# A fused block-sparse attention and low-rank mixer kernel: casts of U and V and the changeover reordered, and q, k, v of the later head pairs loaded by casting transfers

## The chip, the cores and the metric

One Trainium2 chip, one core. The core has a matrix engine (PE, with its weight loads shown apart as PEld), a vector engine (DVE), a scalar engine for activations (ACT), GpSimd (POOL) and SyncE (SP), which here only issues transfers. Each engine works through its own queue in order. Transfers issued by SP or ACT go out on hardware queues, those issued by POOL on a software queue, whose descriptors POOL's own cores write (SWDGE); all of them run on the same 16 DMA engines. A casting transfer reads one number type and writes another.

The metric is the device time of one execution in microseconds. Before the change: median 285.85 us of 8 runs, from 284.97 to 288.19.

## The reference

The shapes are batch 4, 8 heads, 768 positions, head dimension 64; U is 768 x 32, V 32 x 768, w_ch1 512 x 2048, w_ch2 2048 x 512. All are float32.

```python
scores = scale * np.matmul(q, k.transpose(0, 1, 3, 2))
mask = np.abs(blk_i - blk_j) <= 1        # blocks of 32
mask = mask | (blk_i == 0) | (blk_j == 0) | (blk_i == n_blocks - 1) | (blk_j == n_blocks - 1)
...                                      # and three sampled blocks for each block of queries
scores = np.where(mask, scores, -1000000000.0)
attn = softmax(scores)
x = np.matmul(attn, v)                   # heads side by side: [4, 768, 512]

h = x.transpose(0, 2, 1) @ U @ V
u = x + h.transpose(0, 2, 1)
return u + np.maximum(u @ w_ch1, 0.0) @ w_ch2
```

The mixer works along the positions, so U and V multiply over the 768 positions; the last line is a two-layer network on each position.

## The kernel before

**Pairs, units, batches.** Two heads form a pair (`i`), so there are 16 pairs, four to a batch. The scores of a pair are computed in nine units (`u`), each with two heads by 512 columns into one "double", a PSUM tile of two banks (`psc`). ACT takes the exponential of a unit from PSUM into `est` in fp16 (line 481). All matrix work is in fp16.

**Loading.** `issue` (line 229) has SP load q, k or v of a pair in float32 into `qld`, `kld`, `vld`, two buffers each; the lines of a pair are 1536 contiguous bytes for each partition and head. `cast` (line 235) has POOL convert them: q and k to `qst` and `kst` (two buffers each), v into `vts`, where every head and position tile has 66 columns, 64 of them of v. q and k must then stand with the head dimension on partitions. For pairs 0 to 5 PE transposes them (`turn_part`, line 918, through PSUM `pturn` and a DVE copy); for pairs 6 to 15 SP issues a DMA transpose (`turn_dma`, line 261).

**Batch 0** (loop at line 1025, pairs 0 to 3) is a fixed order: at each unit the scores, the values of the unit three earlier (`flush_value`), and what `at_unit` (line 945) hangs on the unit. The mask is added within the scores' matmul there. When the values of a pair are complete, DVE normalizes them into `xs` (line 524), POOL casts `xh` (line 542), PE multiplies by `Ut` (`pa`), DVE copies, PE multiplies by `Vt` (`ph`), DVE adds `xf` (line 628), POOL casts `uh` (line 642), and PE transposes it (`puT`, line 694) for the network. Those steps of pair 0 fall on the units 5 to 7 of pair 1 and unit 0 of pair 2. `Ut` and `Vt` are cast by POOL from float32 loads that lie in the memory of w2t; behind them POOL issues the casting loads of w1t (line 421) and w2t (line 429), placed on units by `WLOADS`.

**The changeover** (lines 1078 to 1115) leaves that order: the first three units of pair 4, the last steps of pair 3, and the first w1 rows of batch 0's network, with `fill` as the list of its steps. The two-bank PSUM tiles grow from two to four when the single-bank pools `pav` and `ps` are given up (`more_doubles`). `put_off` holds the two full `xf` additions of pair 3.

**The stream** (from line 1183) is a planner that runs while the program is built. It keeps estimated clocks for PE, ACT, DVE and POOL (`clk`), and at each step gives PE the next thing whose inputs are due: a unit of scores, the values of a pair (`pav`), the two mixer products, or a step of the network (`pt` for w1 with the relu into `tT`, `pch` for w2). Exponentials, masks (line 502: a multiplication by DVE in batches 1 to 3), relus and additions are placed on ACT and DVE by those clocks. `run_on("pool", us)` advances the planned clock of POOL, and `mask_mul` reckons 1.25 us for a mask if POOL's clock is ahead of DVE's and 0.69 otherwise. Each engine's order is fixed by the time that the kernel runs. `unit_sides` (line 1043) hangs the loads of pair i+3, the casts of pair i+2 and the DMA transposes of pair i+1 on the units of pair i. SP also issues the DMA transposes of `uh` (line 677) and the stores of the result (line 777), whose tile `of` has one buffer.

Of the kernel before, what the change touches and what calls it, by code (L numbers as in the profile page):

```python
# [11 lines left out]
FP16 = mybir.dt.float16  # L12
# [5 lines left out]
P = 128  # L18
# [3 lines left out]
def kernel(  # L22
# [12 lines left out]
    nc = tc.nc  # L35

    B, H, S, D = q.shape
    BLK = 32
    NB = S // BLK
    T = S // P  # L40
    HD = H * D
    HP = H // 2
# [92 lines left out]
    def later(eng, first, fn, when=None):  # L135
        count[0] += 1
        when = clk["pe"] if when is None else when
        tasks[eng].append((when + LAG, first, count[0], fn))

    def run_engines(t):  # L140
        while True:
            best = None
            for eng in ("act", "dve"):
                for kind in (eng, "any"):
                    for task in tasks[kind]:
                        start = max(clk[eng], task[0])
                        late = 0.15 if kind == "any" and eng == "dve" else 0.0
                        key = (start + late, task[1], task[2])
                        if start <= t and (best is None or key < best[0]):
                            best = (key, eng, kind, task, start)  # L150
            if best is None:
                return
            _, eng, kind, task, start = best
            tasks[kind].remove(task)
            clk[eng] = start
            clk[eng] += task[3](eng)

    def more_doubles(tag, n):
        first[tag].__exit__(None, None, None)
        pool = ctx.enter_context(  # L160
            tc.tile_pool(
                name=f"double{n}p", bufs=1, space=bass.MemoryType.PSUM,
                side="left" if tag == "ps" else "right",
            )
        )
        doubles[n] = (pool, clk["pe"])

    def run_on(eng, us, ready=None):
        clk[eng] = max(clk[eng], (clk["pe"] if ready is None else ready) + LAG) + us
        return clk[eng]  # L170
# [46 lines left out]
    NPAIR = B * HP  # L217
# [11 lines left out]
    def issue(i, names="qkv"):  # L229
        if i >= NPAIR:  # L230
            return
        for nm in names:
            keep(nc.sync.dma_start(out=new_ld(i, nm), in_=src_of(nm, i)))

    def cast(i, nm):
        if i >= NPAIR:
            return
        b, hp = divmod(i, HP)
        ld = lds.pop((i, nm))
        if nm == "v":  # L240
            keep(
                nc.gpsimd.tensor_copy(  # L242
                    out=vts[b % 2][:, 2 * hp : 2 * hp + 2, :, 0:D], in_=ld
                )
            )
            return
        st = stpool.tile([P, T, 2, D], FP16, tag="st" + nm, name=nm + "st")
        keep(nc.gpsimd.tensor_copy(out=st.rearrange("p t h d -> p h t d"), in_=ld))  # L248
        sts[i, nm] = st

    def turn_some(st, pt, t0, t1):
        for t in range(t0, t1):
# [665 lines left out]
    def turn_part(i, nm, part):  # L918

        if part == 0:  # L920
            turning[nm] = pst_tile([P, T, P], FP16, "pturn", tag="ps")
        turn_some(sts[i, nm], turning[nm], 3 * part, 3 * part + 3)
        if part == 1:
            del sts[i, nm]
            pt = turning.pop(nm)
            if i < HP:
                dst = {"q": qa, "k": ka}[nm][i % 2]
                for h in range(2):
                    half_copy(nc.vector.tensor_copy, dst, h, pt, 0, T)
            else:  # L930
                qkT[i, nm] = qkpool.tile([P, T, P], FP16, tag=nm + "T", name=nm + "T")
                keep(nc.vector.tensor_copy(out=qkT[i, nm], in_=pt))
            run_on("dve", 0.48)
# [8 lines left out]
    }  # L942


    def at_unit(i, u):
        if (i, u) in MASKS:
            mask_tiles(MASKS.index((i, u)))
        if i == 0:
            if u == 0:
                warm_pe(1)  # L950
                turn_some(qst, pq, TQ, T)
                turn_some(kst, pk, TK, T)
                for h in range(2):
                    mask_rows("dve", h, pm2[:, 0, 0:QB], QA, S)
                    keep(
                        nc.sync.dma_start(
                            out=qa[1][h][mrows[h], :], in_=qa[0][h][mrows[h], :]
                        )
                    )
                    hot_rows(nc.sync, 1, h, D)  # L960
                for nm, o, pt, t in (("q", qa[0], pq, TQ), ("k", ka[0], pk, TK)):
                    for h in range(2):
                        half_copy(nc.vector.tensor_copy, o, h, pt, t, T)
                for h in range(2):
                    keep(nc.sync.dma_start(out=mvld[h * R : h * R + R], in_=moe_V))
                keep(
                    nc.sync.dma_start(
                        out=uld, in_=moe_U.rearrange("(p t) r -> p (t r)", t=T)
                    )
                )  # L970
                issue(2, "qk")
                cast(1, "q")
                cast(1, "k")
                cast(1, "v")
            if u == 1:
                issue(2, "v")
            if u == 3:
                for r in range(2):
                    at = r * R
                    keep(  # L980
                        nc.gpsimd.tensor_copy(
                            out=Ut[rows[r]].rearrange("p t (h c) -> p t h c", h=2)[
                                :, :, :, at : at + R
                            ],
                            in_=uld[rows[r]]
                            .rearrange("p (t r) -> p t r", t=T)[:, :, None, :]
                            .broadcast_to([D, T, 2, R]),
                        )
                    )
                keep(  # L990
                    nc.gpsimd.tensor_copy(
                        out=Vt[0 : 2 * R, :, :],
                        in_=mvld.rearrange("r (p t) -> r t p", t=T),
                    )
                )
                issue(3)
            if u == 6:
                cast(2, "q")
                cast(2, "k")
                cast(2, "v")  # L1000
            if u == 4:
                turn_part(1, "q", 0)
                turn_part(1, "q", 1)
            if u in (5, 6):
                turn_part(1, "k", u - 5)
            return
        if u == 0:
            issue(i + 3)
        if i == 2 and u == 0:
            for h in range(2):  # L1010
                keep(nc.sync.dma_start(out=Vd[rows[h]], in_=Vt[rows[0]]))
        if (i, u) in WLOADS:
            WLOADS[i, u]()
        if u in (1, 2, 3, 4):
            turn_part(i + 1, "qk"[(u - 1) // 2], (u - 1) % 2)
        if u == 6:
            cast(i + 2, "q")
            cast(i + 2, "k")
        if u == 8:
            cast(i + 2, "v")  # L1020
        for _ in range({0: 1, 5: 2, 6: 1, 7: 1}.get(u, 0)):
            if tails:
                tails.popleft()()
# [19 lines left out]
    def unit_sides(i, u):  # L1043

        if u == 0 and i > HP:
            turn_dma(i + 1, "q")
            turn_dma(i + 1, "k")
        if u in (1, 4, 6):
            issue(i + 3, "qkv"[u // 3])
        if u in (3, 5, 7):  # L1050
            cast(i + 2, {3: "q", 5: "k", 7: "v"}[u])
            run_on("pool", 1.15)

    def next_unit(held_back=False):
        i, u = stream.popleft()
# [16 lines left out]
    def run_fill():  # L1072
        cost, fn, kind = fill.popleft()
        fn()
        state["last"] = clk["pe"]
        return cost
# [3 lines left out]
    for gi in range(3):  # L1080
        next_unit(True)
        if gi == 0:
            flush_value()
            tails.popleft()()
            flush_value()
        if gi == 1:
            flush_value()
            put_off.pop(0)()
        if gi == 2:
            tails.popleft()()  # L1090
            tails.popleft()()
            put_off.pop(0)()


    fill.extend(mlp_steps(0))
# [4 lines left out]
    tails.popleft()()  # L1100
    run_fill()
    tails.popleft()()
    for _ in range(5):
        run_fill()
        run_engines(1e9)
    while put_off:
        put_off.pop(0)()
    more_doubles("pav", 2)
    for nm in "qk":
        for part in range(2):  # L1110
            turn_part(HP + 1, nm, part)
    clk["pe"] = clk["dve"] = max(clk["act"], clk["pe"])
    more_doubles("ps", 3)
    for mask in early:
        later("dve", 3, mask, 0.0)

    opened, credit = 1, 0.0
    uT_at = {b: [] for b in range(B)}
# [115 lines left out]
```

## Time and profile before

| | |
|---|---|
| median of 8 runs | 285.85 us (284.97 to 288.19) |
| the profiled execution | 286.49 us, of which the span of the engines' work is 284.7 us |
| granted PE clock | 1.00 in every stretch |
| transfers of q, k, v by SP | 48 tensors, 384 KB each; median landing 5.2 to 5.6 us |
| casting loads by POOL | w1t 4 x 512 KB written, landing 9.7 us; w2t 4 x 512 KB, 18.5 us |
| DMA transposes | 10 of q, 10 of k, 12 of uh |
| POOL casts of q, k, v | 15.2, 15.1 and 17.3 us busy (15, 15 and 16 casts) |
| DMA share, 94 to 120 us | 0.74 |

Times are in microseconds from the start of the span. A row of a timeline gives start, duration, engine, source line, operation, what it writes and reads, and in brackets how long the engine was idle before it and what ended that. A row of the chain gives start, duration and what the end of the execution hung on at that time. SPq and POOLq stand for an engine's issuing of transfers.

### The profile page before, as it was taken

How to read it: one execution, taken by the hardware profiler on the slowest of the kernel's cores; microseconds unless marked ns; L12 is line 12 of the kernel's file. 1: busy time of each engine (PE TensorE's matmuls, PEld its weight loads, DVE VectorE, ACT ScalarE, POOL GpSimd, SP SyncE). 2: the span in 40 equal slices, each digit the busy share in tenths (PEclk: the TensorE clock that was granted, in tenths of full speed). 3: DMA queues.
4: the chain of work that ended last, by engine and by line, in shares of the span. 5: the costliest groups of instructions: out<-in, count | busy, mean ns of one | idle time of the engine just before them, and what ended most of it. 6: DMA issues, size and time to landing. Idle time of an engine off the chain costs nothing.

```text
span 284.7 us, 8067 instructions
## 1 busy us (share of the span) xinstructions
PE 275.6 (97%) x3509; PEld 164.8 (58%) x3509; DVE 182.6 (64%) x285; ACT 178.7 (63%) x201; POOL 85.5 (30%) x102
## 2 busy tenths in 40 slices
PE   8989999799999999999999999999999999999996
PEld 3567775456565656666656464656565554665443
DVE  5657768767879898986776949886867551000112
ACT  3789997397969685775794757496878200655000
POOL 2459863201526263332242525161102011000000
PEclk9999999999999999999999999999999999999999
DMA  5969999928173596665245383913100303100112
GB/s 165 273 207 351 235 252 268 269 57 223 30 222 51 150 223 230 113 215 116 83 110 141 100 227 105 183 24 63 23 9 2 101 2 104 74 1 2 74 74 75
DMA packets 45235, 37.20 MB, mean 131 GB/s; under 512 B 27144, under 2 KB 42832, under 8 KB 45200
## 3 DMA queue, kind: packets, MB, share of 16 engines
q1 hardware_dynamic: 42024, 32.26, 41.2%
q0 software_dynamic: 2688, 4.19, 8.0%
q8 instruction: 27, 0.44, 0.6%
q10 hardware_dynamic: 488, 0.24, 0.3%
q14 instruction: 8, 0.07, 0.1%
HBM read 27.90 MB, written 6.29 MB: 120 GB/s over the span
## 4 chain that ended last, share of the span: by engine, by line
PE 79%; DMA 7%; ACT 7%; DVE 2%; POOL 2%; issue 1%; SPq 0%; ACTq 0%; DVEq 0%; POOLq 0%
PE pch L174 29%; PE pt L174 29%; PE pav L174 10%; PE psc L174 8%; ACT est L481 7%; DMA kld<-in_k_dram 3%; DMA vld<-in_v_dram 2%; DMA w2t<-in_moe_U_dram 1%; PE pa L174 1%; PE ph L174 1%; DVE tT L721 1%; POOL w1t L421 0%; DVE xh L524 0%; DVE est L502 0%; PE pturn L254 0%
## 5 line engine op out<-in xcount | busy, mean ns | idle before, releaser
L481 ACT ACTIVATE est<-psc 128x1024 f16<-128x1024 f32 x144 | 142.6, 1029 | 45.0 <-PE psc L174 42.6
L174 PE MATMUL pt<-uT,w1t 64*128 64x384 f16 (+1 forms) x896 | 95.6, 324 | 1.0 <-ACT est L481 0.5
L502 DVE TENSOR_TENSOR est<-est,m 128x1024 f16<-128x1024 f16 x108 | 87.1, 835 | 12.1 <-ACT est L481 11.5
L174 PE MATMUL pch<-w2t,tT 64*128 64x512 f16 (+3 forms) x688 | 93.4, 372 | 0.5 <-ACT est L481 0.5
L174 PEld LDWEIGHTS <-w1t 64*128 64x128 f16 (+1 forms) x896 | 46.6, 94 | 37.3 <-PE pt L174 7.0
L174 PEld LDWEIGHTS <-tT 64*128 64x128 f16 (+1 forms) x688 | 38.4, 95 | 38.3 <-PE pch L174 1.6
L719 ACT ACTIVATE tT<-pt 128x768 f16<-128x768 f32 (+1 forms) x50 | 38.6, 779 | 32.0 <-PE pt L174 31.9
L174 PEld LDWEIGHTS <-est 128*128 128x128 f16 x1152 | 41.5, 97 | 11.0 <-issue 5.0
L174 PE MATMUL pav<-vt,est 128*128 128x65 f16 x1152 | 44.5, 193 | 0.2
L774 DVE TENSOR_TENSOR of<-xf,pch 128x1024 f32<-128x1024 f32 (+3 forms) x16 | 15.2, 953 | 43.4 <-PE pch L174 43.3
L174 PE MATMUL psc<-qT,kT 64*128 64x512 f16 (+1 forms) x288 | 40.7, 323 | 0.0
L581 POOL CAST xh<-xs 128x768 f16<-128x768 f32 x12 | 11.1, 923 | 94.9 <-DVE xs L572 84.1
L667 POOL CAST uh<-xf 128x768 f16<-128x768 f32 x12 | 13.4, 1118 | 32.8 <-DVE xf L658 17.2
L174 PE MATMUL psc<-qa,ka 128*128 128x512 f16 (+1 forms) x96 | 22.0, 331 | 0.2
L174 PEld LDWEIGHTS <-kT 64*128 64x128 f16 x288 | 14.5, 94 | 11.0 <-DVE xs L572 0.2
L721 DVE TENSOR_SCALAR tT<-pt 128x768 f16<-128x768 f32 (+1 forms) x18 | 16.3, 910 | 5.1 <-PE pt L174 5.1
L242 POOL CAST vt<-vld 128x768 f16<-128x768 f32 x16 | 17.3, 1082 | 5.8 <-DMA vld<-in_v_dram 5.8
L248 POOL CAST kst<-kld 128x768 f16<-128x768 f32 x15 | 15.1, 1009 | 4.2 <-DMA kld<-in_k_dram 3.0
L248 POOL CAST qst<-qld 128x768 f16<-128x768 f32 x15 | 15.2, 1012 | 2.0 <-DMA qld<-in_q_dram 2.0
L658 DVE TENSOR_TENSOR xf<-xs,ph 128x768 f32<-128x768 f32 x12 | 11.4, 953 | 2.3 <-PE ph L174 2.0
L572 DVE TENSOR_TENSOR xs<-pav,rcp 128x768 f32<-128x768 f32 x12 | 11.5, 958 | 1.2
L570 DVE RECIPROCAL rcp<-pav 128x12 f32<-128x12 f32 x12 | 2.8, 232 | 12.8 <-PE pav L174 12.8
(65 smaller groups left out, 127.3 us busy)
## 6 DMA issues: line engine op xcount, KB each, us to landing
vld<-in_v_dram SPq DMA_DIRECT2D x16, 384.0 KB, 5.2
qld<-in_q_dram SPq DMA_DIRECT2D x15, 384.0 KB, 5.4
kld<-in_k_dram SPq DMA_DIRECT2D x15, 384.0 KB, 5.6
out_dram<-of SPq DMA_DIRECT2D x9, 512.0 KB, 3.3
w1t<-in_moe_w_ch_dram POOLq DMA_DIRECT2D x4, 512.0 KB, 9.7
w2t<-in_moe_w_ch_dram POOLq DMA_DIRECT2D x4, 512.0 KB, 18.5
out_dram<-of SPq DMA_DIRECT2D x5, 256.0 KB, 2.0
qld<-in_q_dram SPq DMA_DIRECT2D x1, 256.0 KB, 2.8
```

The source lines that it names most:

```text
L174: ins = nc.tensor.matmul(out, lhsT, rhs, start=start, stop=stop, skip_group_check=loose)
L242: nc.gpsimd.tensor_copy(out=vts[b % 2][:, 2 * hp : 2 * hp + 2, :, 0:D], in_=ld)
L248: keep(nc.gpsimd.tensor_copy(out=st.rearrange("p t h d -> p h t d"), in_=ld))
L481: keep(nc.scalar.activation(out=est, in_=psc, func=AF.Exp, scale=0.125))
L502: keep(nc.vector.tensor_tensor(out=o, in0=o, in1=m, op=ALU.mult))
L572: nc.vector.tensor_tensor(out=xs.rearrange("p (c j) (h d) -> p c (j h) d", c=2, h=2), in0=pv[:, :, :, 0:D], in1=rcp[:, :, :, None].broadca ...
L581: keep(nc.gpsimd.tensor_copy(out=xh, in_=xs))
L658: nc.vector.tensor_tensor(out=u.rearrange("p (c j) n -> p c j n", c=2), in0=xs.rearrange("p (c j) n -> p c j n", c=2), in1=ph[:, :, 0:HS]. ...
L667: keep(nc.gpsimd.tensor_copy(out=uh, in_=u))
L719: keep(nc.scalar.activation(out=o, in_=i, func=AF.Relu))
L721: keep(nc.vector.tensor_scalar_max(out=o, in0=i, scalar1=0.0))
L774: nc.vector.tensor_add(out=of, in0=xfs[b][:, sc : sc + nsc, n0:n1], in1=pch)
```

## The change

1. The casts of U and V are taken apart. `cast_U` goes from unit 3 to unit 6 of pair 0, ahead of q and k of pair 2; `cast_V`, with the cast of v of pair 2, goes to unit 2 of pair 1. Both turns of k of pair 1 are at unit 6, and the four turns of pair 2 come one unit later than before.
2. `issue(i + 3)` stops with pair 5. For pairs 6 to 15, `load_cast` has POOL issue two casting transfers for each of q, k and v (one for each head), straight into `qst`, `kst` and `vts`. The planner's clock of POOL is no longer advanced for them.
3. q and k of pair 5 are turned by DMA transposes instead of by PE. In the changeover four network steps come after the additions and masks are handed to the planner, and the clocks are set otherwise; the planner's order after that point differs in many places.

```diff
+    def load_cast(i, nm):
+
+        if i >= NPAIR:
+            return
+        b, hp = divmod(i, HP)
+        if nm == "v":
+            o = vts[b % 2][:, 2 * hp : 2 * hp + 2, :, 0:D]
+        else:
+            sts[i, nm] = stpool.tile([P, T, 2, D], FP16, tag="st" + nm, name=nm + "st")
+            o = sts[i, nm].rearrange("p t h d -> p h t d")
+        for h in range(2):
+            keep(nc.gpsimd.dma_start(out=o[:, h], in_=src_of(nm, i)[:, h]))
...
+    def cast_U():
+        for r in range(2):
...
+    def cast_V():
+        keep(
+            nc.gpsimd.tensor_copy(
+                out=Vt[0 : 2 * R, :, :],
+                in_=mvld.rearrange("r (p t) -> r t p", t=T),
+            )
+        )
...
             if u == 3:
-                for r in range(2):
...
                 issue(3)
             if u == 6:
+                cast_U()
                 cast(2, "q")
                 cast(2, "k")
-                cast(2, "v")
             if u == 4:
                 turn_part(1, "q", 0)
                 turn_part(1, "q", 1)
-            if u in (5, 6):
-                turn_part(1, "k", u - 5)
+            if u == 6:
+                turn_part(1, "k", 0)
+                turn_part(1, "k", 1)
             return
-        if u == 0:
+        if u == 0 and i < 3:
             issue(i + 3)
+        if i == 1 and u == 2:
+            cast_V()
+            cast(2, "v")
...
-        if u in (1, 2, 3, 4):
-            turn_part(i + 1, "qk"[(u - 1) // 2], (u - 1) % 2)
+        at = u - 2 if i == 1 else u - 1
+        if at in range(4):
+            turn_part(i + 1, "qk"[at // 2], at % 2)
...
-        if u in (1, 4, 6):
-            issue(i + 3, "qkv"[u // 3])
         if u in (3, 5, 7):
-            cast(i + 2, {3: "q", 5: "k", 7: "v"}[u])
-            run_on("pool", 1.15)
+            load_cast(i + 2, {3: "q", 5: "k", 7: "v"}[u])
...
             put_off.pop(0)()
+            turn_dma(HP + 1, "q")
+            turn_dma(HP + 1, "k")
...
-    for _ in range(5):
-        run_fill()
-        run_engines(1e9)
+    run_fill()
+    clk["act"] = clk["pe"]
+    clk["dve"] = clk["pe"] + 0.5
     while put_off:
         put_off.pop(0)()
-    more_doubles("pav", 2)
-    for nm in "qk":
-        for part in range(2):
-            turn_part(HP + 1, nm, part)
-    clk["pe"] = clk["dve"] = max(clk["act"], clk["pe"])
-    more_doubles("ps", 3)
     for mask in early:
         later("dve", 3, mask, 0.0)
+    for _ in range(4):
+        run_fill()
+    more_doubles("pav", 2)
+    more_doubles("ps", 3)
+    run_engines(clk["pe"])
```

In batch 0's part of the built program POOL's order around the change is: `Ut`, q and k of pair 2, two `xh` of pair 0, `Vt`, v of pair 2, two issues of w1t, q and k of pair 3, `uh`, w1t, `uh`. Before, `Vt` stood behind `Ut`, and the two `xh` behind v of pair 2.

More of the change, by code (lines that the diff above doesn't have):

```diff
@@ L942 @@
     }
+    def cast_U():
+        for r in range(2):
+            at = r * R
+            keep(
+                nc.gpsimd.tensor_copy(
+                    out=Ut[rows[r]].rearrange("p t (h c) -> p t h c", h=2)[
+                        :, :, :, at : at + R
+                    ],
+                    in_=uld[rows[r]]
+                    .rearrange("p (t r) -> p t r", t=T)[:, :, None, :]
+                    .broadcast_to([D, T, 2, R]),
+                )
+            )
+    def cast_V():
+        keep(
+            nc.gpsimd.tensor_copy(
+                out=Vt[0 : 2 * R, :, :],
+                in_=mvld.rearrange("r (p t) -> r t p", t=T),
+            )
+        )
     def at_unit(i, u):
@@ L977, in at_unit @@
             if u == 3:
-                for r in range(2):
[L979 to L995, printed above, removed]
                 issue(3)
             if u == 6:
+                cast_U()
                 cast(2, "q")
                 cast(2, "k")
-                cast(2, "v")
             if u == 4:
```

## The prediction

> **What bounds the kernel now.** I read the page first: the sum of busy time, then the chain of work that ended last.
>
> ```profile
> span 284.7 us, 8067 instructions
> PE 275.6 (97%) x3509; PEld 164.8 (58%) x3509; DVE 182.6 (64%) x285; ACT 178.7 (63%) x201; POOL 85.5 (30%) x102
> PE 79%; DMA 7%; ACT 7%; DVE 2%; POOL 2%; issue 1%; SPq 0%; ACTq 0%; DVEq 0%; POOLq 0%
> ```
>
> PE ends the kernel, but an average hides three stages. From 9.5 to 48 us, batch 0, ACT runs one exponential after another and the chain is ACT's; from 48 to 56 us lies a changeover in which PE and ACT both pause; from 56 us on PE is dense (27.4 of 28.0 us busy in 66 to 94, 32.0 of 32.0 in 150 to 182), so there only less PE work or a stall moves the end. Next, the chain of waits between 17 and 30 us, where batch 0 leaves ACT:
>
> ```profile
> 17.07 5.18 DMA vld<-in_v_dram
> ...
> 22.30 0.83 POOL vt L242
> ...
> 25.20 0.83 POOL qst L248
> 26.03 0.76 POOL kst L248
> 26.79 0.45 POOL uh L642
> 27.23 0.46 POOL w1t L421
> 27.70 0.52 POOL uh L642
> ...
> 28.27 0.34 PE puT L694 x3
> 28.61 0.45 PE psc L174 x2
> ```
>
> The reader should see that POOL, a third busy overall, is here the engine that ends last: the load of v for pair 2 lands, POOL works through its queue without a pause, and PE's transposes of uh (puT) for pair 0, with the scores behind them, wait for its last cast. Then the timelines of POOL and PE at the places that the change rewrites:
>
> ```profile
> 17.80 1.56 POOL L991 CAST Vt<-w2t 64x768 f16<-64x768 f32 x1
> 19.31 0.82 POOL L248 CAST qst<-qld 128x768 f16<-128x768 f32 x1
> 21.31 0.83 POOL L248 CAST kst<-kld 128x768 f16<-128x768 f32 x1 [1.19 <-PE pav L174]
> 20.18 0.34 PE L254 MATMUL pturn<-id,qst 128*128 128x128 f16 x3 [1.03 <-POOL qst L248]
> 54.04 0.51 PE L254 MATMUL pturn<-id,qst 128*128 128x128 f16 x6 [1.58 <-DVE xf L628]
> 55.66 0.39 PE L174 MATMUL psc<-qT,kT 64*128 64x512 f16 x2
> ```
>
> The cast of Vt delays q of pair 2, and PE waits 1.03 us for it. But Vt also fills a pause of POOL, which has to wait for k of pair 2 anyway.
>
> **Part 1, order in batch 0.** Vt's cast (one, 1.56 us) goes from ahead of q and k of pair 2 to behind the two xh of pair 0; the turns of pair 2 come one unit later. I follow POOL's new queue by starts of the rows above. q of pair 2 was issued at 15.06 and landed 3.4 later, so its cast runs at 18.5 and is ready at 19.3; its turn now comes after 20.4, so the 1.03 us wait goes. k was issued at 15.54 and landed 5.6 later, 21.14. From there, start to start: k 0.77, two xh 0.90, Vt 1.51, v 0.77, two issues of w1t 1.21, q and k of pair 3 1.54, uh 0.45, w1t 0.52, uh 0.52: 8.19 us, so the last uh ends at 29.3. Before, it ended at 28.2. PE, freed of its earlier wait, reaches puT a microsecond sooner and waits there longer; what follows (psc, then the exponential that began at 29.13) begins at about 30.2. Price: **+1.1 us**, and both old pauses (ACT's 0.89 before 21.00 and 0.36 before 29.13) lie ahead of this point and bring nothing. Bounds: -1.2 if POOL's order should hurt nobody (0.89 + 0.36 gained), +1.6 if the whole of Vt is added.
>
> **Part 2, the changeover.** Twelve PE transposes for pair 5 (2 x 0.51 us) and two DVE copies (0.56, 0.55) go; two DMA transposes on SP replace them. Their inputs were cast by 42 us and their result is read at pair 5's first scores, past 62 us; the median landing of such transposes is 4.4 and 3.1 us, and SP has only pair 6's loads there, which go. If that cover failed, pair 5's scores would wait. PE's run of pt now goes from 14 to 22 matmuls without the stall on xf. At 0.65 us for eight (chain rows "pt x8") 22 take 1.8 from 51.00: 52.8. The scores then need the PSUM that ph held; DVE reads it in xf, 1.02 us straight behind the uT copy that ended at 51.46: 52.5. So the scores of unit 3 of pair 4 start at 52.9 instead of 55.66: **-2.7 us**. ACT has the four relu halves first (1.75 us from 52.3) and the next exponential at 54.0 instead of 56.1, so it follows. Bounds: -3.0 to -1.0; the low gain if DVE, with nine masks, two half and three whole relus (9 x 0.69 + 1.02 + 2.85) from 51.5 on, delays pair 4's values.
>
> **Part 3, loads that cast.** For pairs 6 to 15, 30 loads leave SP (0.37 to 0.57 us of issuing each) and 30 casts leave POOL (1.08, 1.01, 1.01 us); 60 casting issues of 192 KB read come to POOL.
>
> ```profile
> L429 POOL DMA_DIRECT2D w2t<-in_moe_w_ch_dram x4 | 3.0, 746 | 0.0
> L421 POOL DMA_DIRECT2D w1t<-in_moe_w_ch_dram x4 | 2.3, 572 | 0.0
> q0 software_dynamic: 658, 0.65, 64.2%
> q1 hardware_dynamic: 781, 0.19, 32.7%
> ```
>
> The first two rows are casting issues of 512 and 128 pieces; each new one has 768 (128 partitions x 6 tiles). The slope gives 0.86 us; bounds 0.57 (no slope) and 1.12 (all in proportion). Per pair POOL gives 3.1 us of casts for 5.2 of issues and has, with xh and uh (0.92, 1.12), 7.2 us of work in a pair's 14.3 us (values of pair 4 at 65.94, of pair 13 at 194.55, nine pairs). Behind xh stand four issues, 3.4 us, then uh, whose input came 4.5 us after xh's start at pair 5 (83.40 to 87.93): it fits up to 0.92 us an issue, beyond which uh is late. That moves PE only where uh opens the next batch's w1 rows (pairs 7 and 11).
>
> The last two rows are the DMA view of 42 to 48 us (casting packets, 1024 bytes written: 0.642 x 16 x 6 us / 658 = 94 ns, few short ones among them) and of 75 to 78 us (transposes, 256 bytes: 0.327 x 48 / 781 = 20 ns). Each pair will bring 4608 packets of 128 bytes written, 288 an engine, for 48 of 1536 bytes. Cost of one: between 20 and 94 ns. It is nearest to the 256-byte row in size. The trace's records of single packets say the same more finely: medians of 18 ns for that row, 96 for casting ones of 1024 bytes and 322 for those of 4096 (w1t); the line through the two casting points gives 30 ns at 128 bytes, which I take. Then 8.6 us a pair for loads, 2.9 for three transposes (144 x 20 ns), about 1 for stores: 12.5 of 14.3 us. It fits. The trade-off: k lands later. At pair 8 POOL's xh ends at 84.2, four issues end at 87.6, and with the 5.6 us landing of a plain kld counted from the last issue (86.8) k is there at 92.4, against an SP transpose at 91.78 before. SP then holds its queue 0.6 us, and stores (98.89) and uT (103.63) behind it lose nothing; kT is read 14 us later. DVE's masks that ran at up to 1.31 us beside a POOL cast instead of 0.69 get quicker, without value where PE is dense. Price: **0**.
>
> The Trainium skill, "DMA: Bandwidth & Descriptors", Specifications, speaks against the part: transfers need at least 512 bytes for line rate, below that the engine reads, modifies and writes. The 20 ns row at 256 bytes shows no such penalty for that write. Were it to double 128-byte packets from my 30 ns to 60, an estimate, loads would need 17.3 us a pair and the third rival below would hold.
>
> **The sum**: +1.1 - 2.7 + 0 = -1.6. The profiled execution took 286.49 (span 284.7, 1.8 around it): 284.9. It lies 0.64 above the median of 285.85, so as a median **284.3 us**. About 0.5% (1.4 us, so below 284.4 or above 287.3) is what a measurement of this kernel can tell from no change; my forecast sits on that line.
>
> **Rivals.** *Batch 0 gains too.* POOL's queue is not what holds PE after the move, because casts shorten or PE has work to hide it; then -1.2 - 2.7: 282.0. For it: the 1.03 us wait is real and goes. Against: the chain shows POOL without a pause for 6 us before puT. *The gain is given back.* PE reaches 53 us sooner but the denser first units wait for DVE masks or for relus to free PSUM, so 1.0 stays: 286.0 with Part 1's +1.1. For it: DVE works 10.5 of 13 us in 53 to 66 even before; against: PE then had no pause over 0.25 us. *Loads become the bound* (slower): packets on the 16 DMA engines. It decides from (14.3 + 14.3/10 - 3.9) / 288 = 41 ns a packet, since a lead of about one pair over ten pairs is used up first. At 45 ns, 13.0 + 3.9 = 16.9 a pair: 10 x 2.6 - 14 = +12, 296. For it: 128-byte pieces, v at a stride of 132 bytes, no row of either; against: both nearest rows. *The change doesn't do what it says* is excluded: the built program shows the order and the 60 issues.
>
> **Numbers.** Forecast 0.45 (own range 283.0 to 285.6; 0.24 of it below 284.4, 0.21 within), batch 0 gains too 0.17 (faster), given back 0.20 (half within, half slower), loads bound 0.18 (slower). Faster 0.41, same 0.31, slower 0.28. The range starts below the first rival, 281.5, and goes to 289.0: the second rival with an issue at its upper bound, where uh is late by 4 x (1.12 - 0.92) = 0.8 us at pairs 7 and 11, plus the top of Part 1 (+0.5) fits in; the third lies outside.
>
> **What would show it.** Part 1: no wait of PE on qst near 20 us, a wait of over 1.5 us at puT near 27 to 29 us, the exponentials after it from about 30.2. Part 2: no pturn near 54 us, unit 3's scores at about 52.9 + 1.1. Part 3: about 47,000 packets on the software queue, near 30 ns each, issues near 0.86 us, DMA share near 0.9 in 66 to 190 us, and no new PE wait. I am wrong if puT does not wait, if PE has waits of over 2 us past 60 us, or if packets take over 41 ns.

## The result and the profile after

The changed kernel takes 283.49 us (median of 20 runs, 282.32 to 284.73) against 285.81 us (55 runs of the kernel before): ratio 0.9912, 95% interval 0.9896 to 0.9929, a gain of 2.0 to 3.0 us. Ratios are of fast runs alone (order only and its repeat had one slow run each), so they can differ a little from the quotient of the medians. The profiled execution took 284.73 us, the slowest of the 20, and its first stage is among the longest of the twelve profiles that are compared below. The page:

```profile
span 282.9 us, 8050 instructions
PE 274.8 (97%) x3497; PEld 163.6 (58%) x3497; DVE 175.0 (62%) x285; ACT 177.3 (63%) x199; POOL 100.2 (35%) x132
q0 software_dynamic: 49728, 10.10, 45.9%
q1 hardware_dynamic: 35464, 20.85, 35.4%
PE 79%; DMA 7%; ACT 6%; POOL 3%; DVE 1%; issue 1%; SPq 1%; ACTq 0%; DVEq 0%; POOLq 0%
```

The reader should see that PE lost only the twelve transposes (3509 to 3497 instructions), DVE 7.6 us of work although its count of instructions is the same, and that POOL is busier, not less. The software queue's share rose from 8.0% to 45.9%.

**Batch 0.** POOL's timeline of the changed kernel, and below it PE's and ACT's rows behind it:

```profile
20.84 0.83 POOL L248 CAST kst<-kld 128x768 f16<-128x768 f32 x1 [1.58 <-DMA kld<-in_k_dram]
21.61 0.96 POOL L555 CAST xh<-xs 128x384 f16<-128x384 f32 x2
22.51 1.56 POOL L974 CAST Vt<-w2t 64x768 f16<-64x768 f32 x1
24.02 0.82 POOL L242 CAST vt<-vld 128x768 f16<-128x768 f32 x1
...
28.53 0.52 POOL L655 CAST uh<-xf 128x384 f16<-128x384 f32 x1
```

```profile
29.10 0.34 PE L707 MATMUL puT<-id,uh 128*128 128x128 f16 x3 [0.64 <-POOL uh L655]
```

```profile
29.97 17.18 ACT L494 ACTIVATE est<-psc 128x1024 f16<-128x1024 f32 x18 [1.35 <-PE psc L174]
```

and ACT's row at the same place in the kernel before:

```profile
29.13 17.16 ACT L481 ACTIVATE est<-psc 128x1024 f16<-128x1024 f32 x18 [0.36 <-PE psc L174]
```

The last uh ends at 29.05 (28.21 before), PE waits for it, and the eighteen exponentials begin at 29.97 (29.13 before). PE's wait on qst near 20 us is gone in this execution. In the list of PE's waits the two at puT come to 1.0 us together.

**The changeover**, in PE's timeline of the changed kernel:

```profile
51.84 2.11 PE L174 MATMUL pt<-uT,w1t 64*128 64x384 f16 x22
53.79 0.38 PE L174 MATMUL psc<-qT,kT 64*128 64x512 f16 x2
```

The run of 22 pt stands where 14, a stall on xf and the transposes stood. The scores of unit 3 start at 53.79, against 55.66 before, though batch 0's exponentials ended 0.86 later: relative to that end 2.73 us earlier.

**The stream.** The masks on DVE and the three groups of casting issues (busy us, mean ns of one | idle us before them, and what ended most of it), then the table of the stretch from 94 to 120 us (width, then busy time and instructions of PE, PEld, DVE, ACT, POOL, then granted clock, DMA share, GB/s):

```profile
L515 DVE TENSOR_TENSOR est<-est,m 128x1024 f16<-128x1024 f16 x108 | 78.7, 745 | 17.2 <-ACT est L494 16.0
L262 POOL DMA_DIRECT2D qst<-in_q_dram x20 | 16.3, 819 | 0.1
L262 POOL DMA_DIRECT2D vt<-in_v_dram x20 | 16.3, 820 | 0.0
L262 POOL DMA_DIRECT2D kst<-in_k_dram x20 | 16.3, 819 | 0.0
94.00:120.00 26.00, 25.91 (x390) 15.33 (x388) 21.05 (x31) 17.02 (x18) 14.37 (x17) 1.00 1.33 135
```

The masks and the same stretch in the kernel before:

```profile
L502 DVE TENSOR_TENSOR est<-est,m 128x1024 f16<-128x1024 f16 x108 | 87.1, 835 | 12.1 <-ACT est L481 11.5
94.00:120.00 26.00, 25.53 (x402) 15.79 (x401) 22.90 (x30) 18.10 (x19) 11.23 (x10) 1.00 0.74 182
```

Masks take 745 ns in the mean (835 before), an issue takes 0.82 us, and the DMA share is 1.33 (0.74 before). It passes 1.00, so packets overlap on an engine and the time of each is counted; in half rows (below) the software queue alone has 1.31 in this stretch. In the trace's records of single packets the 46,080 casting ones have a median of 32 ns (mean 36.6). PE is busy 25.91 of 26.00 us all the same, and past 60 us it has two waits, of 0.4 and 0.2 us.

**Where the time went.** Four marks cut every profile of this study into stretches: the end of the long row of exponentials of batch 0 (29.97 + 17.18 here), the first pav x72 of the chain (63.53), the start of its last pt x128 (237.74), and the end of the span.

| profile | batch 0 ends at | changeover takes | stream takes | close takes |
|---|---|---|---|---|
| before | 46.29 | 19.65 | 174.29 | 44.5 |
| changed | 47.15 | 16.38 | 174.21 | 45.2 |
| changed, again | 44.89 | 16.38 | 174.21 | 45.2 |
| order only | 46.25 | 16.69 | 175.31 | 44.9 |
| order only, again | 47.46 | 16.39 | 175.29 | 44.9 |
| loads only | 44.98 | 19.65 | 175.36 | 45.1 |
| old changeover | 45.49 | 19.16 | 174.08 | 45.2 |
| old batch 0 | 47.16 | 16.39 | 174.24 | 45.2 |
| Vt between | 45.37 | 16.40 | 174.23 | 45.2 |
| Vt between, again | 45.27 | 16.39 | 174.25 | 45.2 |
| half rows | 46.20 | 16.38 | 175.98 | 44.7 |
| casts kept | 45.84 | 16.39 | 175.85 | 44.7 |

Changeover and stream repeat within 0.1 us wherever the program there is the same, with one changeover at 16.69 (order only, where PE waits 0.67 us at 61.01 for a transpose of k). Batch 0 does not: one and the same program ended it at 47.15 and at 44.89. So the table is read by its two middle columns, and batch 0 is judged only by many runs. The changed kernel gains 3.27 in the changeover and nothing in the stream, and loses 0.7 at the close, behind the last matmul and the last addition; -2.6 in sum, against -2.5 measured by the ratio.

### The profile page after: what moved, and what is told of

It reads as the page before. It is cut to its first block, busy times and chain, and to the rows that moved or that the text cites. A ratio compares the mean times of both kernels' runs of the same rounds, so it can differ in the third digit from the quotient of the medians.

```text
span 282.9 us, 8050 instructions
## 1 busy us (share of the span) xinstructions
PE 274.8 (97%) x3497; PEld 163.6 (58%) x3497; DVE 175.0 (62%) x285; ACT 177.3 (63%) x199; POOL 100.2 (35%) x132
## 3 DMA queue, kind: packets, MB, share of 16 engines
q0 software_dynamic: 49728, 10.10, 45.9%
## 4 chain that ended last, share of the span: by engine, by line
PE 79%; DMA 7%; ACT 6%; POOL 3%; DVE 1%; issue 1%; SPq 1%; ACTq 0%; DVEq 0%; POOLq 0%
PE pt L174 29%; PE pch L174 28%; PE pav L174 10%; PE psc L174 8%; ACT est L494 6%; DMA kld<-in_k_dram 4%; DMA vld<-in_v_dram 3%; PE pa L174 2%; POOL xh L594 1%; PE ph L174 1%; SPq L233 1%; POOL w1t L434 1%; POOL vt L242 1%; DVE xh L537 0%; DVE xs L585 0%
## 5 line engine op out<-in xcount | busy, mean ns | idle before, releaser
L174 PE MATMUL pt<-uT,w1t 64*128 64x384 f16 (+1 forms) x896 | 94.6, 324 | 0.5 <-ACT est L494 0.4
L515 DVE TENSOR_TENSOR est<-est,m 128x1024 f16<-128x1024 f16 x108 | 78.7, 745 | 17.2 <-ACT est L494 16.0
L174 PEld LDWEIGHTS <-tT 64*128 64x128 f16 (+1 forms) x688 | 37.8, 95 | 38.4 <-PE pch L174 1.4
L732 ACT ACTIVATE tT<-pt 128x768 f16<-128x768 f32 (+1 forms) x48 | 36.8, 776 | 33.7 <-PE pt L174 33.7
L174 PE MATMUL pav<-vt,est 128*128 128x65 f16 x1152 | 44.5, 193 | 0.1
L734 DVE TENSOR_SCALAR tT<-pt 128x768 f16<-128x768 f32 (+1 forms) x20 | 18.2, 916 | 4.6 <-PE pt L174 4.3
L262 POOL DMA_DIRECT2D qst<-in_q_dram x20 | 16.3, 819 | 0.1
L262 POOL DMA_DIRECT2D vt<-in_v_dram x20 | 16.3, 820 | 0.0
L262 POOL DMA_DIRECT2D kst<-in_k_dram x20 | 16.3, 819 | 0.0
```

The lines of the kernel that those rows point to most:

```text
L174: ins = nc.tensor.matmul(out, lhsT, rhs, start=start, stop=stop, skip_group_check=loose)
L262: keep(nc.gpsimd.dma_start(out=o[:, h], in_=src_of(nm, i)[:, h]))
L515: keep(nc.vector.tensor_tensor(out=o, in0=o, in1=m, op=ALU.mult))
L732: keep(nc.scalar.activation(out=o, in_=i, func=AF.Relu))
L734: keep(nc.vector.tensor_scalar_max(out=o, in0=i, scalar1=0.0))
```

## The experiments

Each was timed against the kernel before on the same chip. "Order" below means the order of PE, DVE and ACT in the built program.

**Order only.** The changed kernel with the old float32 loads by SP and casts by POOL for pairs 6 to 15; the order is the changed kernel's, which was planned without these casts on POOL's clock.

```diff
-        if u == 0 and i < 3:
+        if u == 0:
             issue(i + 3)
...
+        if u in (1, 4, 6):
+            issue(i + 3, "qkv"[u // 3])
         if u in (3, 5, 7):
-            load_cast(i + 2, {3: "q", 5: "k", 7: "v"}[u])
+            cast(i + 2, {3: "q", 5: "k", 7: "v"}[u])
```

> The changed kernel with the old loads for pairs 6 to 15: float32 transfers by SP and casts by POOL again, while PE, DVE and ACT keep the changed kernel's order instruction for instruction. Theory (the loads are worth nothing, batch 0's order costs 0.8 to 1.1 us and the changeover gives 2.7): 283.5 us, within 0.6 us of the changed kernel. Rival A (the loads bring the gain, since masks no longer run beside POOL casts): near 285.8. Rival B (the loads cost about 1 us on crowded DMA engines, which the order hides): 282.5.

Measured: 284.44 us, ratio 0.9940 (0.9911 to 0.9968). It holds most of the gain; the stream is 1.1 us longer than with the casting loads.

**Loads only.** The kernel before with the casting loads alone, in the order of before, which was planned with the old casts on POOL's clock (`load_cast` is added as in the change, `run_on` for POOL stays).

```diff
-        if u == 0:
+        if u == 0 and i < 3:
             issue(i + 3)
...
-        if u in (1, 4, 6):
-            issue(i + 3, "qkv"[u // 3])
         if u in (3, 5, 7):
-            cast(i + 2, {3: "q", 5: "k", 7: "v"}[u])
+            load_cast(i + 2, {3: "q", 5: "k", 7: "v"}[u])
```

> The kernel before with only the casting loads for pairs 6 to 15; PE, DVE and ACT keep the order of before instruction for instruction. Theory: 285.8 us, no change beyond 0.6 us; DMA share rises from 0.5 to 0.7 towards 1.0 and more in 66 to 182 us, casting packets at 32 to 37 ns, no new wait of PE. Rival A: 283.5. Rival B: 286.8.

Measured: 287.03 us, ratio 1.0035 (1.0011 to 1.0059): slower by 0.3 to 1.7 us. The stream is 1.07 longer although masks run at 749 ns. Nearly all of it arises between two pairs' values: 27.05 us from 105.66 to 132.71, against 26.01 before (106.96 to 132.97). PE's timeline shows where most of it lies:

```profile
121.34 0.34 PE L174 MATMUL pt<-uT,w1t 64*128 64x384 f16 x2 [0.86 <-DMA uT<-uh]
```

SP had issued that transpose at 115.71, so it took about 5.6 us to land, and PE was ready for it 4.8 us after the issue. uT landed in a median of 2.8 us before and in 4.4 in this run (4.9 in the changed kernel). With the casting packets the transfers with a short lead land later, and in the old order one of them comes too late. That this wait is the whole of the loss was not tried by itself.

**Vt between.** The changed kernel with Vt's cast between q and k of pair 2, in the pause in which POOL waits for k; only POOL's order differs.

```diff
                 cast_U()
                 cast(2, "q")
+                cast_V()
                 cast(2, "k")
...
-            cast_V()
             cast(2, "v")
```

> The changed kernel with the cast of Vt between the casts of q and k of pair 2, in the pause of 1.58 us that POOL has there; only POOL's order changes. Theory (POOL's queue from k of pair 2 to uh of pair 0 holds PE at puT): the last uh ends some 1.4 us earlier, PE does not wait at puT, the exponentials after it begin at about 28.8 instead of 29.97, and the kernel takes 282.3 us. Rival (PE would have been held by something else there): 283.5, no change.

Measured: 283.16 us, ratio 0.9896 (0.9855 to 0.9936). The interval contains the changed kernel's, so it was taken again beside that kernel (below).

**Old changeover.** The changed kernel with the changeover of before.

```diff
             put_off.pop(0)()
-            turn_dma(HP + 1, "q")
-            turn_dma(HP + 1, "k")
...
-    run_fill()
-    clk["act"] = clk["pe"]
-    clk["dve"] = clk["pe"] + 0.5
+    for _ in range(5):
+        run_fill()
+        run_engines(1e9)
     while put_off:
         put_off.pop(0)()
...
+    for nm in "qk":
+        for part in range(2):
+            turn_part(HP + 1, nm, part)
+    clk["pe"] = clk["dve"] = max(clk["act"], clk["pe"])
     more_doubles("ps", 3)
```

> The changed kernel with the changeover of before: pair 5 turned by PE and DVE, every relu and addition handed out before the masks, clocks set as before. Theory (the changeover is worth 2.7 us to the changed kernel): 286.2 us, and the scores of unit 3 of pair 4 start about 2.7 us later than the 53.79 of the changed kernel. Rival (the changeover's gain is taken back by DVE and ACT in the next 10 us): 284.0.

Measured: 286.23 us, ratio 1.0003 (0.9974 to 1.0031). Without the new changeover the whole gain is gone: it is worth 0.0091 x 285.8 = 2.6 us here, and the column of the changeover says 19.16 - 16.38 = 2.78. Its two halves, the turns of pair 5 by DMA and the new order of its steps, were not tried apart. The stream, with casting loads and an order of its own, takes 174.08. PE has its old wait back, in the list of waits of this run:

```profile
PE pturn L267 <- DVE xf L641: 1.6, 1, 1.6
```

**Changed kernel again**, with no edit, beside the next two.

> The changed kernel itself once more, so that its neighbours of this call are compared with it on one chip. 283.5 us; between executions its start may differ by about a microsecond, as the landings of the first loads do.

Measured: 283.38 us, ratio 0.9896 (0.9858 to 0.9935).

**Vt between, again**, the same program as above.

> Vt's cast in POOL's pause between q and k of pair 2, again, beside the changed kernel itself. Theory (POOL's queue holds PE at puT in most executions): 1.0 to 1.4 us below the changed kernel, 282.3. Rival (that wait of 1.35 us of ACT belongs to the profiled execution alone, where loads landed late): within 0.4 us of it.

Measured: 283.25 us, ratio 0.9900 (0.9860 to 0.9940), 0.13 us from the changed kernel on the same chip. My order of POOL's casts there cost nothing that these runs could see; they could not have told half a microsecond (their intervals reach about 1.1 us each way).

**Old batch 0.** The changed kernel with batch 0's old order: Vt beside Ut, v of pair 2 with q and k, the turns a unit earlier.

```diff
             if u == 6:
-                cast_U()
                 cast(2, "q")
                 cast(2, "k")
+                cast(2, "v")
...
-        if i == 1 and u == 2:
-            cast_V()
-            cast(2, "v")
...
-        at = u - 2 if i == 1 else u - 1
-        if at in range(4):
-            turn_part(i + 1, "qk"[at // 2], at % 2)
+        if u in (1, 2, 3, 4):
+            turn_part(i + 1, "qk"[(u - 1) // 2], (u - 1) % 2)
```

(`Ut` and `Vt` are cast at unit 3 of pair 0 again, as in before.)

> The changed kernel with batch 0's order of before: Vt ahead of q and k of pair 2, turns of pairs 1 and 2 at their old units; changeover and casting loads as changed. Theory (Part 1 costs 0.8 to 1.1 us net): 282.6 us, PE waits for qst near 20 us and hardly at puT. Rival (Part 1 gains 0.9, since the wait for qst is the larger one): 284.5.

Measured: 283.62 us, ratio 0.9906 (0.9872 to 0.9940), 0.24 from the changed kernel on the same chip, inside the intervals. The waits of PE in this run's profile and in that of the changed kernel again, in this order, each with total, count and longest:

```profile
PE pturn L267 <- POOL qst L248: 3.0, 1, 3.0
```

```profile
PE puT L707 <- POOL uh L655: 0.6, 1, 0.6
PE pturn L267 <- POOL qst L248: 0.6, 1, 0.6
```

With the old order this one execution waits 3.0 us for q of pair 2, where the profile of before waited 1.0. With the new order the changed kernel has a 0.6 us wait on qst in one execution and none in the other. What holds PE in batch 0 changes from execution to execution, with the landings of the first loads: over the twelve profiles SP issued q of pair 2 anywhere from 12.40 to 15.09 us, and batch 0 ended at 44.98 to 47.16 with the old order and at 44.89 to 47.46 with the new one.

**Half rows.** The changed kernel with every casting transfer split into two halves of the columns: 120 issues, 92,160 packets of 64 bytes written.

```diff
         for h in range(2):
-            keep(nc.gpsimd.dma_start(out=o[:, h], in_=src_of(nm, i)[:, h]))
+            for c in range(2):
+                cols = slice(c * D // 2, (c + 1) * D // 2)
+                keep(
+                    nc.gpsimd.dma_start(
+                        out=o[:, h, :, cols], in_=src_of(nm, i)[:, h, :, cols]
+                    )
+                )
```

> The changed kernel with every casting transfer split by columns into two: 128-byte reads and 64-byte writes, 576 packets an engine and pair instead of 288, and 12 issues instead of 6. It asks how far the DMA engines and POOL are from the limit. At 26 to 30 ns a packet loads alone take 15 to 17 us of an engine in a pair's 14.3, POOL 2.0 + 12 x 0.82 = 11.8. Theory (the 16 engines are nearly full, past their limit the loads bound the stream): slower by 10 us or more, 294 or above, with PE waiting for kT or uT. Rival (there is plenty of room): within 2 us of the changed kernel.

Measured: 284.82 us, ratio 0.9953 (0.9923 to 0.9983), 1.4 above the changed kernel on the same chip. The same stretch as above, and the two largest waits in the stream:

```profile
94.00:120.00 26.00, 24.51 (x364) 14.03 (x361) 20.04 (x29) 15.26 (x17) 22.90 (x28) 1.00 2.01 144
```

```profile
PE pa L174 <- POOL xh L600: 1.1, 3, 0.8
PE psc L174 <- DMA kT<-kst: 0.7, 1, 0.7
```

The share reaches 2.01 and PE is still busy 24.51 of 26.00 us. The casting packets have a median of 27 ns, little under the 32 ns of those twice as large. POOL is now nearly full (22.90 of 26.00), and the loss is a late xh and a late k, once, between 89.59 and 103.47 (13.88 us between two pairs' values, 12.12 in the changed kernel); ahead of and behind that place the values come at the changed kernel's distances.

**Casts kept.** The changed kernel with a useless cast of a q-sized tile on POOL behind each pair of casting issues; PE, DVE, ACT and SP keep their order. This and the next run ask which half of the old loading cost 1.1 us in order only.

```diff
             load_cast(i + 2, {3: "q", 5: "k", 7: "v"}[u])
+            if i + 2 < NPAIR:
...
+                a, b = [s.rearrange("p h t d -> p (h t d)") for s in scratch]
+                keep(nc.gpsimd.tensor_copy(out=b.bitcast(FP16)[:, 0:S], in_=a))
```

> The changed kernel with a cast on GpSimd put back behind each pair of casting issues for pairs 6 to 15 (128 x 768 float32 to fp16, on two idle tiles, so its result goes nowhere); PE, DVE, ACT and SP keep the changed kernel's order. The stream from the first to the last batch's values took 174.2 us with the casting loads and 175.3 in the one profile with float32 loads and casts in the same order. If the casts make that difference (they slow the masks of DVE beside them, 835 against 745 ns in the mean, and make xh late), masks return to about 830 ns, the stream to about 175.3 and the time to 284.4 (ratio 0.994 to 0.996). If SP's float32 loads make it (they stand ahead of the transposes on SP's queue), masks may slow down but the stream stays at 174.2 and the time at 283.4 (ratio 0.990 to 0.992). I lean to the second: PE is dense there, and slower masks were hidden before.

Measured: 284.63 us, ratio 0.9959 (0.9937 to 0.9981): the interval lies wholly above the changed kernel's. The stream took 175.85 and the masks 936 ns. My lean was wrong: casts on POOL bring the loss back with SP's float32 loads gone; whether those loads cost something as well was not tried alone. POOL's whole load is higher here than in order only, since the issues stay (21.86 of 28.00 us busy from 66 to 94, against 12.20), so the size of the loss, 1.64 in the stream, is not that of the old casts. One thing here I can't explain: by the trace 11 masks ran beside issues (for 0.3 us or more) and no cast, and 6 of them took over 1 us, where none of 32 such masks did in the changed kernel.

**Order only, again**, the same program as order only.

> The changed order with float32 loads and casts for pairs 6 to 15 once more, beside the kernel with casts put back on the same chip. If casting loads are worth something in the new order, it is 0.9 us or so slower than the changed kernel again (284.4, ratio 0.994), with a stream near 175.3 us. If the first run's profile was one execution's accident, the stream is 174.2 and the ratio 0.991, and the casting loads are worth nothing, as forecast.

Measured: 284.65 us, ratio 0.9927 (0.9893 to 0.9961), stream 175.29. The longer stream repeats; by the ratios, 0.9940 and 0.9927 against 0.9912 and 0.9896, the difference is 0.4 to 1.3 us, with overlapping intervals. All of the stream's difference arises in two pairs: the values from the first to the third pair of the stream take 28.07 us (63.85 to 91.92) against 27.00 in the changed kernel (63.53 to 90.53), the rest 147.2 in both. The chain near 85 us in order only, again, two masks and a wait of PE before 74 us, the casts of POOL beside the chain, and the masks on DVE between 64 and 91 us in this run and in the changed kernel:

```profile
82.58 2.57 DVE est L515 x2
85.15 0.21 DVE a L623
85.36 0.02 issue
85.38 0.30 DVE a L624
85.68 0.04 issue
85.72 0.34 PE ph L174 x6
```

```profile
68.79 2.27 DVE L515 TENSOR_TENSOR est<-est,m 128x1024 f16<-128x1024 f16 x2
73.11 0.39 PE L174 MATMUL psc<-qT,kT 64*128 64x512 f16 x2 [0.26 <-DVE tT L734]
```

```profile
82.55 0.83 POOL L594 CAST xh<-xs 128x768 f16<-128x768 f32 x1 [6.11 <-DVE xs L585]
83.32 1.29 POOL L248 CAST qst<-qld 128x768 f16<-128x768 f32 x1
```

```profile
L515 DVE TENSOR_TENSOR est<-est,m 128x1024 f16<-128x1024 f16 x18 | 17.2, 988 | 0.5 <-ACT est L494 0.4
```

```profile
L515 DVE TENSOR_TENSOR est<-est,m 128x1024 f16<-128x1024 f16 x19 | 14.3, 779 | 1.8 <-ACT est L494 1.5
```

Two masks beside two casts take 2.57 us; a mask alone takes 0.68 in the same timeline. Behind them stand the two steps that make `a`, and PE's ph waits for these. That is about half of the 1.1 us. The other half arises near 73 us in the same way: two masks beside two casts take 2.27 us (1.28 in the changed kernel), a relu (tT) stands behind them, and PE waits for it. In the changed kernel the same place has the chain on PE throughout, because POOL has issues there and not casts (82.52 to 85.77): two masks take 1.95, since the second is not slowed.

The Trainium skill, "SBUF — State Buffer", section "Who interferes with whom", has a rule for this: DVE and GpSimd share one pair of SBUF ports as an exclusive lock, and by the section "SBUF: two separate sides" a DVE operation with two SBUF inputs takes it against a GpSimd operation that reads SBUF. The mask is such an operation and the cast reads SBUF; 745, 825 to 835 and 936 ns without the loading casts, with them and with casts on top of issues agree with it. So do single pairs of the changed kernel, in which the first to start keeps its time and the other is held up:

```profile
94.32 0.69 DVE L515 TENSOR_TENSOR est<-est,m 128x1024 f16<-128x1024 f16 x1
94.37 1.33 POOL L594 CAST xh<-xs 128x768 f16<-128x768 f32 x1 [4.01 <-DVE xs L585]
```

```profile
138.76 0.83 POOL L680 CAST uh<-xf 128x768 f16<-128x768 f32 x1 [2.48 <-issue]
138.81 1.32 DVE L515 TENSOR_TENSOR est<-est,m 128x1024 f16<-128x1024 f16 x1 [0.17 <-ACT est L494]
```

Of the 24 masks that overlap a cast there, the 12 that began before it took 0.68 to 0.69 us and the 12 that began after it 0.78 to 1.35. So a cast beside a mask cost DVE nothing where the mask was ahead.

## Why the prediction came out as it did

The forecast of 284.3 us lay 0.8 above the measured 283.49; its sum of -1.6 compares with -2.5 by the ratio.

**Part 2, the changeover: right.** Forecast -2.7 us. The trace has -2.73 at unit 3 of pair 4, old changeover against changed has 2.78 in that stretch and 2.6 by the ratios. No pturn and no wait on xf are left near 54 us. The start at 52.9 plus 1.1 is 54.0, and it came at 53.79.

**Part 1, batch 0: the mechanism seen in one execution, the price not.** The term was +1.1 us with the exponentials from about 30.2. In the one profiled execution it shows: last uh at 29.05 (forecast 29.3), exponentials from 29.97, 0.84 later than before, qst's wait gone. PE waited 1.0 at puT in two pieces where I said over 1.5 in one. But over executions it is worth nothing that can be measured: old batch 0, Vt between and the changed kernel lie within 0.4 us (283.62, 283.25, 283.38 on one chip). The step that failed was to take the chain of one execution as the chain of the median. The loads that I started POOL's queue from (15.06 and 15.54) shift between executions (q of pair 2 by up to 2.7 us), and with them what holds PE: sometimes qst, sometimes uh, sometimes neither. With Part 1 at 0 the sum would have been -2.7, against -2.5 by the ratio, so this term can be the whole of the 0.8 us; but the intervals of these runs reach about 1 us each way, and a part worth half a microsecond, up or down, would not show. That the rest adds up is luck in part: 0.49 in the changeover that comes without its edit (19.65 to 19.16) and the 0.7 at the close, neither of which I had, about cancel.

**Part 3, the loads: 0 came out, but over two terms that I had not seen.** The stream is 174.29 before and 174.21 after. In the new order the old casts make it 175.3: DVE has only 0.5 us of idle time before masks between 64 and 91 us there (0.9 before), and PE waits for what stands behind slow masks. That is of the second rival's kind, a gain given back to masks, but that rival gave back 1.7 of the 2.7 in the first units, and this is 1.1, later on. The casting loads took the casts off POOL, and that brought the 1.1 us back. The step that failed is "DVE's masks ... get quicker, without value where PE is dense": in the new order PE is dense only because masks are quick. On the old order the loads cost 1.0 us, a late landing most of it.

Both losses have one thing in common that the experiments do not take apart: each order was planned for its own loading, the old one with the casts on POOL's clock and the new one without, and each lost 1.0 to 1.1 us with the other's. With orders of their own the streams take 174.29 (casts), 174.08 and 174.21 (casting loads). So between kernels that are each planned for their loading the loads may be worth nothing, as forecast; the new changeover with the old loads and with POOL's clock advanced for them was not tried. As the orders stand, the two parts are worth more together than the sum of each alone: -1.7 or -2.1 (order only) and +1.0 (loads only) make -0.7 to -1.1, against -2.5.

Of its details: an issue 0.82 us (forecast 0.86), a packet 32 ns in the median (30), share 1.02 to 1.33 in the four stretches from 66 to 182 us (0.9: the mean packet, 36.6 ns, is longer, and transposes' packets went from 23.9 to 34.1 ns in the mean). The transpose of k of pair 8 was issued at 89.93, ahead of the 92.4 at which I had k arrive; that of pair 9 came late (6.5 us behind q's, at 103.83), and nobody read it late. No new wait of PE over 0.4 us appeared past 60 us, as forecast.

**The third rival** did not happen, but its condition was wrong as well. I added up the times of packets as if an engine took them one after the other, so that the loads became the bound from a share of about 1. Half rows, with the packets doubled and the share at 2.01, lost 1.4 us and not the steadily growing lag that rival implied; its two waits of PE are for a cast of POOL, which had little time left, and for k. The rule of the Trainium skill ("DMA: Bandwidth & Descriptors", Specifications) that the prediction weighed against this part, that below 512 bytes the engine reads, modifies and writes, shows as no doubling here: a casting packet of 128 bytes took 32 ns, near the 30 of the line through my two longer ones.

**The first rival** (282.0, both waits of batch 0 regained) asks for 1.2 us that no run shows beyond the start's own spread; its gain of 3.9 us in all lies outside the measured 2.0 to 3.0.

**Open:** the close of the kernel is 44.5 us in the one profile of before and 44.7 to 45.2 in the eleven others. Whether the casting loads, the order or chance adds this was not tried. Open as well are the two halves of the changeover, the new order planned for the old loads, and the slow masks beside issues in casts kept.

## What to carry to other kernels

Before a wait near the start of a kernel is priced, look at more than one execution: a chain that begins with a load's landing is one draw, and a reordering that only trades which late load is waited for may be worth nothing in the median.
Work that leaves GpSimd can have a value on DVE: count the DVE operations that start while it runs, and ask after each other edit whether DVE still has the idle time that hid them.
Test parts of a change in both directions, alone and left out, since a part that costs alone (+1.0 us here) can be what lets another part keep its gain. Where an order was planned for one part, plan it anew before you price the part's absence.

## What the runs showed of the hardware

- A casting transfer of 768 pieces occupies POOL for 0.82 us, whether a piece is 256 bytes read and 128 written or goes to a stride of 132 bytes (v). In the changed kernel the 32 masks that ran beside issues alone stayed near 0.69 us; beside casts two took 2.57 in order only, again.
- Casting packets have medians of 32 ns at 128 bytes written and 27 ns at 64 bytes, so halving a packet saves about a sixth of its time.
- The busy share of the DMA engines, as the page counts it, is no utilisation: it went to 2.01 in half rows with PE busy 24.51 of 26.00 us and one transpose late, by 0.7 us.
- The cost of these packets to others is latency, and how much depends on the order. In the old order (before, loads only) the median landing of a DMA transpose went from 4.4 to 4.6 us for q, 3.1 to 3.8 for k and 2.8 to 4.4 for uT; in the new one (order only, changed) from 4.2 to 6.4, 3.1 to 4.5 and 2.8 to 4.9.
